# A linear-recurrence attention ahead of two expert layers: a redrawn order of the attention's steps, and inputs laid out time step first

## The chip, the cores and the metric

The kernel runs on one core of a Trainium2 chip. The metric is the device time of one execution in microseconds (us). The engines in the profile are PE (matrix multiplies; PEld its weight loads), DVE (vector), ACT (scalar, activations), POOL (GpSimd) and SP, which here only issues DMA transfers.

## The reference

Three parts run one after the other; the output of each is the next one's input.

```python
def _attn_ref(q, k, v, a_re, a_im):          # each (4, 8, 768, 48): batch, head, time, channel
    mag = np.sqrt(a_re * a_re + a_im * a_im)
    scale = np.minimum(mag, 0.999) / (mag + 1e-06)
    a_re_n, a_im_n = (a_re * scale, a_im * scale)
    for t in range(S):                       # a recurrence over 768 time steps
        new_re = ar * S_re - ai * S_im
        new_im = ar * S_im + ai * S_re
        S_re, S_im = (new_re + k_t v_t^T, new_im)
        y[:, :, t] = q_t S_re
```

Then `x`, the result as 3072 tokens of 384 values, goes through two mixtures of experts: each token takes the one of 8 experts with the highest gate value, `gate * (relu(x @ w1[e]) @ w2[e])`, with `w1` 384 x 1024 and `w2` 1024 x 384. The second layer's gate has a bias that depends on the token's modality.

## The kernel before

**Tiling.** The recurrence is computed in chunks of 128 time steps, as a masked product: within a chunk the decays become cumulative sums of logarithms and angles (matrix multiplies with a triangular matrix, L233), q and k are scaled by the resulting factors, and q k^T under a mask times v gives the chunk's part; a 112-row state `st` carries the rest to the next chunk. Two chunks of one batch element (all 8 heads, 2 x 384 = 768 columns) make a unit; there are 12 units, three for each batch element. Tiles have 128 partitions (time steps) and 384 columns for a chunk or 768 for a unit.

**Steps.** A unit's work is cut into named steps. Those that the text speaks of:
- `ldar`, `ldai`, `ldq`, `ldk`, `ldv` load the inputs by SP's DMA queue (L187); `ck` (L192), `sq1`, `sq3`, `ad` (L202), `su` (L214), `lh`/`ll` (L218 to L221), `th`/`tl` (L228, L230), `tt` (L208) turn the decay into logarithm and angle, 768 columns at a time;
- `pT`, `pL` are the cumulative sums on PE (L233), `fi` and `f` take the angle's fraction (L242, L245), `cf` a few corner rows of it (a cast, L261, and a subtraction, L262);
- `qR` and `kR` scale q and k by the magnitudes (L265, L267), 768 columns;
- `hqc`, `hqs`, `hkc`, `hks` multiply q and k by cosine and sine (L280), 384 columns, with the chunk's number 0 or 1 behind the name. In the trace they are `qhb<-q,fi` (hqc), `qhb<-q,f` (hqs), `khb<-k,fi` (hkc) and `khb<-k,f` (hks);
- `Tq`, `Tk` transpose on PE, `eq`, `ek` copy the results (L168 on ACT, L169 on DVE), `sc` forms the scores, `A` multiplies them by the mask on DVE (L298), `py` and `pu` multiply by v (L304 to L315), `S` and `Sr` keep the state (L322, L347);
- `xe` copies py, `pt` transposes it back, `ye` copies that into `yt`, `st_` stores `yt` into x in DRAM by SP (L1092), `lg` reduces the gate values (L1094).

The router of the first expert layer already works beside the attention: batches of tokens (among others `r1acc`, an addition of 8 columns, L476), and after the last one the finish (`rfnt` to `rfbf`, L498 to L502, and on to the index tile `r1idg`, L521), from which the first gather of tokens `xg` on POOL (L762) follows. `ckon` (L1266) is a memset on DVE for a final check; it waits until all stores into x have landed. Also beside the attention, weights of the experts are loaded (`ws`, L741) and split into two 16-bit parts, and dense work for tokens whose expert was guessed runs on PE with the copies `hh` on ACT (L829) and `hl` on DVE (L830).

**What sets the order.** Nothing is scheduled by the compiler in this part. Each step has a number in the table `AT`, to which the unit's number is added; units 0, 1, 10 and 11 have numbers of their own in `AT_OF`. All steps of all units are sorted by it and issued in that order, so each engine's queue, and SP's, is that order cut down to its own steps. An engine executes its queue in order and waits at an instruction whose input isn't there. Unit 0's wide steps are split into halves, `a` and `b`. The table `ENG` says which engine a step runs on where there is a choice: A is ACT, V is DVE, P is POOL.

```python
todo.append((n+AT_OF.get(n,{}).get(nm,AT[nm]),n,nm,f))
...
todo.sort(key=lambda t:t[:3])
```

Of the kernel before, what the change touches and what calls it, by code (L numbers as in the profile page):

```python
# [18 lines left out]
B, H, S, D = 4, 8, 768, 48  # L19
P = 128  # L20
DM = H * D
# [22 lines left out]
    sub=-59.2026, lhb=-59.0997, zw1=-59.0382, zk0=-53.3853, ldqb=-53.3816, kRa=-53.3802, atb=-50.9528, thb=-50.9075, tlb=-50.8802, llb=-50.8716,
    zw2=-50.8688, aba=-48.2571, zw3=-47.5465, ldkb=-45.6871, csa=-45.6746, sna=-45.6585, qRa=-45.6266, abb=-41.2423, zld=-36.0444, csb=-35.4916,
    zw4=-33.8895, snb=-33.8869, ldva=-32.3857, qRb=-28.9291, zk1=-28.5196, zk3=-22.0775, kRb=-20.8793, zk2=-20.375, zwh7=-20.0527, ldvb=-7.6984,
    zwh5=-7.0878, zwh6=-6.1043, ldar=-4.03, zf=-3.5878, ldai=-3.4105, ck=-3.4097, sq1=-3.0855, sq3=-2.9701, ad=-2.6001, ln1=-2.5145, ln2=-2.5138,
    ex3=-2.5125, ex2=-2.4717, su=-2.4082, tt=-2.3592, lh=-2.0144, at=-1.9704, ll=-1.6353, pL0=-1.6327, th=-1.6191, ldq=-1.6042, tl=-1.5858,
    pT0=-1.5524, R0=-1.547, fi0=-1.5398, Ri0=-1.5358, ldv=-1.5354, f0=-1.5216, pL1=-1.5124, pT1=-1.5111, R1=-1.4687, ldk=-1.4045, Ri1=-1.4044,
    fi1=-1.4016, f1=-1.3988, re=-1.1695, cf=-0.9722, qR=-0.971, ab=-0.9699, sn=-0.6365, kR=-0.6337, hks0=-0.6029, hqs0=-0.585, cs=-0.5549,  # L50
    hkc0=-0.5545, hks1=-0.547, hqs1=-0.5433, Tk0=-0.5359, hqc0=-0.5358, Tq0=-0.535, eq0=-0.5124, hkc1=-0.5034, ek0=-0.4694, Tq1=-0.4692, Tk1=-0.4092,
    sc0=-0.4087, hqc1=-0.4036, eq1=-0.4019, ek1=-0.357, A0=-0.3524, Tq2=-0.105, pu0=-0.0199, sc1=-0.0183, pu1=0.0293, Tk2=0.0293, eq2=0.0298,
    py0=0.03, A1=0.0301, zj=0.1705, ek2=0.3622, Tq3=0.3643, py1=0.3651, S0=0.4002, Tk3=0.4007, xe0=0.4077, sc2=0.4092, eq3=0.4092, pu2=0.4188,
    A2=0.4237, ek3=0.4453, pt0=0.4456, pu3=0.4519, ye0=0.4527, sc3=0.4528, lg0=0.4598, py2=0.4639, A3=0.4672, py3=0.4998, xe1=0.5527, S1=0.6012,
    pt1=0.6448, lg1=1.0276, Sr=1.029, st_0=1.0298, ye1=1.4024, dn0=1.5026, st_1=1.9808, dn1=2.6018, zwl6=2.6952, zwh0=9.4349, zx=18.5444, dn2=19.7371,
# [4 lines left out]
    zl1=146.621, zv3=157.976, zn1=162.009, zn2=187.836, zb1=246.1, zn3=246.175, zy=248.185, zp0=248.274, zp1=248.392, zp2=248.534, zp3=248.627,  # L60
    zp4=248.734,)
# [5 lines left out]
        hqs1=-28.8059, eq0=-20.0658, ek0=-19.7488, hqc1=-13.3169, Tq1=-7.6642, pu0=-7.358, pu1=-7.3535, eq1=-6.3712, Tk1=-3.3378, hks1=-3.3077,
        hkc1=-2.9415, S0=-2.7488, ek1=-1.9123, sc0=-1.5685, A0=-1.5614, Tq2=-1.2232, pu2=-1.2102, Tk2=-1.1192, eq2=-1.1182, pu3=-1.115, py0=-1.1141,
        ek2=-1.1137, sc1=-1.1023, A1=-1.0178, Tk3=-0.9703, Tq3=-0.566, ek3=-0.5563, eq3=-0.5149, sc2=-0.5143, A2=-0.5059, py1=-0.4989, xe0=-0.4897,
        sc3=-0.4333, pt0=-0.2777, A3=-0.1413, ye0=0.057, py2=0.1636, py3=0.198, lg0=0.3641, xe1=0.3867, S1=0.4533, Sr=0.4645, pt1=0.5068, lg1=0.5952,  # L70
# [1 line left out]
    1: dict(
        ldar=-122.2447, ck=-118.7214, ldai=-111.041, sq1=-68.5471, ln2=-60.0846, ex2=-56.9239, sq3=-53.2917, ad=-52.0168, tt=-51.9253, at=-47.9791,
        th=-46.6208, ln1=-42.588, ex3=-37.3201, su=-36.2627, lh=-36.1864, tl=-34.871, ll=-34.321, pT0=-34.3209, fi0=-34.3127, pL0=-29.9243,
        f0=-29.9203, R0=-29.5866, Ri0=-22.4378, pL1=-19.6401, R1=-18.0473, Ri1=-16.2534, pT1=-8.6717, fi1=-8.4218, f1=-8.219, ldk=-7.2703,
        ldq=-4.4455, ab=-2.7035, cf=-2.5673, kR=-2.5652, cs=-2.5614, qR=-2.4893, hkc0=-2.2758, sn=-2.225, re=-2.1309, hqs1=-2.0421, hks0=-1.9986,
        hqs0=-1.9704, Tk0=-1.5026, hkc1=-1.5001, ldv=-1.449, ek0=-1.4431, hqc0=-1.4378, Tq0=-1.4305, Tk1=-1.4192, hqc1=-1.4097, hks1=-1.4083,
        eq0=-1.3907, Tq1=-0.8344, ek1=-0.8342, eq1=-0.8097, Tk2=-0.6367, sc0=-0.5888, Tq2=-0.5863, pu0=-0.5203, A0=-0.5192, py0=-0.4913, eq2=-0.4082,
        ek2=-0.4032, Tq3=0.0297, sc1=0.0338, Tk3=0.0387, A1=0.0388, py1=0.3043, xe0=0.4126, eq3=0.4157, S0=0.4162, sc2=0.4256, pt0=0.4496, A2=0.4516,
        pu2=0.4518, ek3=0.4519, sc3=0.457, py2=0.4689, A3=0.4875, py3=0.5219,),  # L80
    10: dict(
        Ri0=-1.5539, ab=-0.9712, eq0=-0.4979, Tk0=-0.4053, ek0=-0.1036, Tk1=0.0277, sc0=0.7494, Tq1=0.7519, pu0=0.7567, ek1=1.4627, A0=1.6015,
        eq1=1.8231, Tk2=1.8243, sc1=1.8248, Tq2=1.9627, py0=4.4609, A1=6.4672, eq2=6.7564, ek2=6.9082, py1=7.0288, Tq3=8.272, sc2=11.6037,
        pu1=11.7032, xe0=11.7276, Tk3=12.5124, eq3=13.1036, ek3=13.1527, S0=13.3673, A2=13.4097, pt0=15.0475, ye0=15.1973, sc3=15.2236, A3=15.2358,
        py2=17.428, pu2=17.4299, lg0=17.4308, py3=18.0597, pu3=26.4085, xe1=26.4185, S1=26.4723, pt1=26.4802, ye1=26.4873, lg1=26.5282, st_0=30.2202,
        Sr=31.9702, st_1=53.6001,),
    11: dict(
        sq3=-3.3998, fi0=-1.536, Ri0=-1.4981, pT1=-1.4279, fi1=-1.2243, pL1=-1.0127, f1=-0.9962, R1=-0.2456, Ri1=0.4687, ab=0.5224, qR=0.5385,
        kR=0.8233, sn=0.8234, cs=1.9193, hqs0=10.7193, hqc0=12.1152, hkc0=12.3445, Tq0=12.503, hks0=12.504, hkc1=13.7743, eq0=13.9012, Tq1=14.1402,
        hqs1=14.177, Tk0=16.9149, ek0=16.9526, eq1=17.0015, hqc1=17.0187, Tq2=25.408, Tk1=25.4086, eq2=25.4698, Tq3=25.5518, sc0=25.5652, pu0=29.219,  # L90
        ek1=29.2192, hks1=29.2197, A0=29.22, Tk2=29.2205, ek2=30.1283, sc1=30.4591, Tk3=31.0328, A1=31.0793, py0=33.9283, sc2=35.3688, pu1=35.4882,
        A2=36.5036, ek3=36.6086, eq3=37.448, py1=37.6666, sc3=38.0008, S0=39.3703, A3=39.3853, xe0=41.3988, pt0=43.479, py2=48.1531, py3=50.2777,
        xe1=51.5924, ye0=51.792, lg0=52.4969, pt1=52.5183, lg1=55.2838, dn0=62.7472, ye1=68.3041, st_0=72.5776, st_1=72.6059, dn1=72.7172, dn2=78.7804,),
# [1246 lines left out]
```

## Time and profile before

| | |
|---|---|
| three runs | 785.13, 785.62 (the median) and 2927.37 us |
| the profiled execution | 784.11 us, span 782.4 us |
| busy over the span | PE 730.3 us (93%), PEld 584.0, DVE 532.9 (68%), ACT 470.1 (60%), POOL 293.1 (37%) |
| DMA | 159260 packets, 91.40 MB, 131804 of the packets under 512 bytes |
| granted clock of PE, mean | 0.981 |

[...] Idle time stands with what ended it, `<-`. L12 is line 12 of the kernel. [...] The first mask multiply of unit 0 starts at 39.68 us, the last `py` ends about 268.0; these two cut the trace into the three stretches used below.

### The profile page before, as it was taken

To read this page: it belongs to the slowest core of one execution; us is meant where nothing else is said; L and a number is where in the kernel's file an instruction comes from. 1 tells how busy PE (TensorE), PEld (TensorE's weight loads), DVE (VectorE), ACT (ScalarE), POOL (GpSimd) and SP (SyncE) were. 2 spreads that over 40 slices of the span, in tenths; PEclk is the share of its full clock that TensorE was granted. 3 is DMA by queue.
4 is the path that set the end of the run, shared out by engine and by line. 5 is a ranking of instruction groups with operands and counts; after the bars stand their busy time and mean duration, and the time that the engine had idled before them with its cause. 6 is when DMAs were issued, how large, how long until landed. Compare 5 with 4: busy or idle time off the path is not lost. (4 is left out here: it accounts for less than half of the span.)

```text
span 782.4 us, 23426 instructions
## 1 busy us (share of the span) xinstructions
PE 730.3 (93%) x8451; PEld 584.0 (75%) x8451; DVE 532.9 (68%) x1415; ACT 470.1 (60%) x1007; POOL 293.1 (37%) x289
## 2 busy tenths in 40 slices
...
GB/s 220 223 149 220 163 159 165 123 164 96 69 70 62 120 146 94 140 134 114 160 87 175 62 196 78 119 103 204 19 59 188 52 53 44 216 49 43 57 49 30
DMA packets 159260, 91.40 MB, mean 117 GB/s; under 512 B 131804, under 2 KB 149764, under 8 KB 159104
## 3 DMA queue, kind: packets, MB, share of 16 engines
...
HBM read 192.54 MB, written 20.84 MB: 273 GB/s over the span
## 5 line engine op out<-in xcount | busy, mean ns | idle before, releaser
L825 PEld LDWEIGHTS <-wh 128*128 128x128 f16 x1296 | 127.3, 98 | 10.9 <-ACTq L891 3.0
L826 PEld LDWEIGHTS <-wh 128*128 128x128 f16 x1296 | 127.3, 98 | 7.3 <-issue 0.5
L827 PEld LDWEIGHTS <-wl 128*128 128x128 f16 x1296 | 127.3, 98 | 0.0
L846 POOL DMA_INDIRECT x<-yo,r1ids x27 | 28.4, 1052 | 191.7 <-ACT hh L829 81.0
L749 DVE SCALAR_TENSOR_TENSOR wl<-ws,wh 128x768 f16<-128x768 f32 x88 | 83.8, 962 | 14.2 <-ACT wh L748 6.7
L748 ACT ACTIVATE wh<-ws 128x768 f16<-128x768 f32 x88 | 74.4, 851 | 10.0 <-ACTq L861 4.8
L838 PEld LDWEIGHTS <-hl 128*128 128x128 f16 x432 | 42.2, 98 | 44.9 <-DVE hl L830 9.5
L838 PE MATMUL mpy<-wh,hl 128*128 128x384 f16 x216 | 70.6, 327 | 3.5 <-DVE hl L830 1.3
L838 PE MATMUL mpu<-wh,hl 128*128 128x384 f16 x216 | 70.5, 327 | 2.7 <-DVE ev L842 1.1
L836 PE MATMUL mpu<-wh,hh 128*128 128x384 f16 x216 | 70.5, 326 | 0.7 <-ACT hh L829 0.6
L836 PE MATMUL mpy<-wh,hh 128*128 128x384 f16 x216 | 70.5, 326 | 0.0
L837 PE MATMUL mpy<-wl,hh 128*128 128x384 f16 x216 | 70.4, 326 | 0.0
L837 PE MATMUL mpu<-wl,hh 128*128 128x384 f16 x216 | 70.4, 326 | 0.0
L846 POOL DMA_INDIRECT out_dram<-yo,r2ids x21 | 21.0, 1002 | 130.1 <-ACT yo L845 115.9
L825 PE MATMUL msc<-xh,wh 128*128 128x128 f16 x384 | 68.5, 221 | 0.9 <-ACTq L891 0.9
L825 PE MATMUL mpk<-xh,wh 128*128 128x128 f16 x384 | 68.0, 220 | 1.3 <-ACTq L891 1.3
L826 PE MATMUL msc<-xl,wh 128*128 128x128 f16 x384 | 68.4, 220 | 0.0
L827 PE MATMUL msc<-xh,wl 128*128 128x128 f16 x384 | 68.4, 220 | 0.0
L830 DVE SCALAR_TENSOR_TENSOR hl<-mpq,hh 128x256 f16<-128x256 f32 x73 | 30.9, 423 | 54.7 <-ACTq L861 21.8
L827 PE MATMUL mpk<-xh,wl 128*128 128x128 f16 x384 | 68.1, 220 | 0.0
L826 PE MATMUL mpk<-xl,wh 128*128 128x128 f16 x384 | 68.0, 220 | 0.0
L825 PE MATMUL mpq<-xh,wh 128*128 128x128 f16 x384 | 67.6, 219 | 0.0
(512 smaller groups left out, 2259.8 us busy)
## 6 DMA issues: line engine op xcount, KB each, us to landing
...
```

The costliest lines, as they stand in the source:

```text
L748: nc.scalar.activation(H_,S_,AF.Copy,scale=WS,accum_out=s.fl[:,s.n:s.n+1]); s.n+=1
L749: if lo: nc.vector.scalar_tensor_tensor(L_,S_,WS,H_,op0=ALU.mult,op1=ALU.subtract)
L825: nc.tensor.matmul(o,W.h1[:,d,fs],x.h[:,d,:],start=(d==0),stop=False)
L826: nc.tensor.matmul(o,W.h1[:,d,fs],x.l[:,d,:],start=False,stop=False)
L827: nc.tensor.matmul(o,W.l1[:,d,fs],x.h[:,d,:],start=False,stop=(d==ND-1))
L830: def hl(q=q): nc.vector.scalar_tensor_tensor(hs[q][2],hs[q][0][:,:,:P],0.0,hs[q][1],op0=ALU.max,op1=ALU.subtract)
L836: nc.tensor.matmul(o,hh[:,r,:],W.h2[:,f,:],start=(f==0),stop=False)
L837: nc.tensor.matmul(o,hh[:,r,:],W.l2[:,f,:],start=False,stop=False)
L838: nc.tensor.matmul(o,hl[:,r,:],W.h2[:,f,:],start=False,stop=(f==NF-1))
L846: nc.gpsimd.indirect_dma_start(out=s.dst,out_offset=bass.IndirectOffsetOnAxis(ap=R.ids[:,j:j+1] if ids is None else ids(),axis=0),in_=y,in ...
```

## The change

1. The five inputs q, k, v, a_re, a_im are handed over as (batch, time, head, channel) instead of (batch, head, time, channel). A load of 128 time steps thus reads 128 rows of 8 x 48 floats (1536 bytes) instead of 128 x 8 rows of 192 bytes. A step's chunks (two in units 1 to 11, one in unit 0's halves) come in one transfer.
2. All numbers in `AT` and `AT_OF` are new. `RING`, `BATCH`, `WARM` stay.
3. In `ENG`, `hkc1`, `hks1`, `hqc1`, `kR` and, in unit 0, `kRb` and `ttb` go from POOL to DVE; `ek1` goes from DVE to ACT and `xe0` from ACT to DVE; `ye0` goes from DVE to ACT and `ye1` from ACT to DVE.
4. A second form of the attention behind a branch (`gen_attention`), which is not taken here, reads the new layout too.

```diff
@@ -37,60 +37,60 @@
 AT=dict(
-    zq3=-275.454, ldarb=-264.9366, zq2=-255.701, ckb=-255.2219, ldara=-254.8635, sq1b=-254.7775, cka=-246.2329, ln2b=-245.3372, sq1a=-186.1661,
...
+    zq3=-158.0658, ldarb=-158.0658, ldara=-158.0657, ldaia=-158.0657, zq2=-156.761, ckb=-156.2861, sq1b=-154.5986, ln2b=-154.0208, zq4=-153.7814,
...
@@ -99,9 +99,9 @@
 ENG=dict(
-    ek2="A", ek3="A", eq0="A", eq1="A", eq2="A", eq3="A", lh="A", sq1="A", sq1a="A", sq3="A", xe0="A", xe1="A", ye1="A", Sr="P", hkc0="P", hkc1="P",
-    hks0="P", hks1="P", hqc1="P", hqs0="P", hqs1="P", kR="P", kRa="P", kRb="P", qR="P", tt="P", ttb="P", ek0="V", ek1="V", hqc0="V", lha="V", lhb="V",
-    qRa="V", qRb="V", sq1b="V", sq3a="V", sq3b="V", th="V", tha="V", thb="V", tta="V", ye0="V",)
+    ek1="A", ek2="A", ek3="A", eq0="A", eq1="A", eq2="A", eq3="A", lh="A", sq1="A", sq1a="A", sq3="A", xe1="A", ye0="A", Sr="P", hkc0="P", hks0="P",
+    hqs0="P", hqs1="P", kRa="P", qR="P", tt="P", ek0="V", hkc1="V", hks1="V", hqc0="V", hqc1="V", kR="V", kRb="V", lha="V", lhb="V", qRa="V", qRb="V",
+    sq1b="V", sq3a="V", sq3b="V", th="V", tha="V", thb="V", tta="V", ttb="V", xe0="V", ye1="V",)
@@ -183,8 +183,8 @@
         def load(nm, src, bufs):
             def ld(_,s,sl):
                 if not hasattr(u,nm): setattr(u,nm,inp.tile([P,HC,H,D],F32,name=nm,tag=nm,bufs=bufs))
-                for c in range(sl.start//DM,sl.stop//DM):
-                    nc.sync.dma_start(out=getattr(u,nm)[:,c],in_=src[b,:,(c0+c)*P:(c0+c+1)*P,:].rearrange("h p d -> p h d"))
+                i,e=sl.start//DM,sl.stop//DM
+                nc.sync.dma_start(out=getattr(u,nm)[:,i:e],in_=src[b,(c0+i)*P:(c0+e)*P].rearrange("(c p) h d -> p c h d",p=P))
@@ -1325,6 +1325,9 @@
     for name in _INS:
...
+        if name in _INS[:5]:
+
+            a = _np.ascontiguousarray(a.transpose(0, 2, 1, 3))
```

How the order moves is seen best where an engine's instructions stand. POOL first, in the middle of the attention: two stretches of one unit each, before

```order
L208 TENSOR_TENSOR x_996<-ai,x_996 128x768
L265 TENSOR_TENSOR q<-q,Rb_154 128x768
L267 TENSOR_TENSOR k<-k,Ri 128x768
L280 TENSOR_TENSOR khb_153<-k,f 128x8x48
L280 TENSOR_TENSOR qhb_150<-q,f 128x8x48
L280 TENSOR_TENSOR khb_153<-k,fi 128x8x48
L280 TENSOR_TENSOR khb_151<-k,f 128x8x48
L280 TENSOR_TENSOR qhb_148<-q,f 128x8x48
L280 TENSOR_TENSOR khb_151<-k,fi 128x8x48
L280 TENSOR_TENSOR qhb_148<-q,fi 128x8x48
```

and with the change:

```order
L208 TENSOR_TENSOR x_1386<-ai,x_1386 128x768
L347 TENSOR_TENSOR st_1368<-st_1368,re 112x384
L265 TENSOR_TENSOR q<-q,Rb_154 128x768
L280 TENSOR_TENSOR khb_151<-k,f 128x8x48
L280 TENSOR_TENSOR khb_151<-k,fi 128x8x48
L280 TENSOR_TENSOR qhb_148<-q,f 128x8x48
L280 TENSOR_TENSOR qhb_149<-q,f 128x8x48
```

The wide multiply k (L267) and three of the seven multiplies of L280 are gone from POOL's unit; the number behind a name tells the tiles of a name apart. They stand on DVE now. A piece of DVE's unit before

```order
L242 TENSOR_SCALAR fi<-pT 128x384
L280 TENSOR_TENSOR qhb_148<-q,fi 128x8x48
L298 TENSOR_TENSOR A<-psc,mask 128x512
L245 TENSOR_TENSOR f<-pT,fi 128x384
L169 COPY kT<-pk 112x512
```

and with the change:

```order
L242 TENSOR_SCALAR fi<-pT 128x384
L245 TENSOR_TENSOR f<-pT,fi 128x384
L280 TENSOR_TENSOR khb_152<-k,fi 128x8x48
L280 TENSOR_TENSOR khb_152<-k,f 128x8x48
L280 TENSOR_TENSOR qhb_149<-q,fi 128x8x48
L214 SCALAR_TENSOR_TENSOR x_1782<-x_1782,x_1772 128x768
L242 TENSOR_SCALAR fi<-pT 128x384
L298 TENSOR_TENSOR A<-psc,mask 128x512
```

Three multiplies in a row stand where one stood, ahead of the mask multiply. The third place is the end of the attention, on SP. Before:

```order
L1092 DMA x<-yt 128x384 x2
L741 DMA ws_90<-in_moe_w_dram 128x3x1024
L1092 DMA x<-yt 128x384 x2
L741 DMA ws_91<-in_moe_w_dram 128x8x384
```

With the change:

```order
L1092 DMA x<-yt 128x384 x2
L741 DMA ws_90<-in_moe_w_dram 128x3x1024
L741 DMA ws_91<-in_moe_w_dram 128x8x384
L1092 DMA x<-yt 128x384
```

The last store of the attention has moved behind both weight loads. The copy that feeds it was on ACT (`ye1`) and is now on DVE, with the change:

```order
L830 SCALAR_TENSOR_TENSOR hl<-mpq,hh 128x256
L169 COPY yt<-pt 128x384
L498 TENSOR_SCALAR rfnt<-mpT 128x8
```

It stands behind the last `hl` and ahead of the router's finish, in which `ckon` has moved from ahead of `rfnt` (L498) to behind `rfbf` (L502).

## Rows read from the trace of the kernel before

**Rows 1.** The same execution in stretches: length, busy time and instructions by engine, PEclk, DMA share, GB/s.

```profile
0.00:39.68 39.68, 27.43 (x175) 14.21 (x176) 35.15 (x73) 32.18 (x50) 22.79 (x48) 0.91 1.10 219
39.68:268.00 228.32, 211.05 (x2450) 177.22 (x2448) 197.06 (x366) 190.65 (x296) 153.33 (x117) 0.96 0.61 126
268.00:782.40 514.40, 491.78 (x5833) 392.61 (x5829) 300.68 (x977) 247.31 (x662) 116.96 (x124) 0.99 0.32 105
```

**Rows 2.** Largest wait of PE, 40 to 260 us: total us, times, longest.

```profile
PE pr L339 <- DVE rtrk L478: 5.9, 2, 2.9
```

**Rows 3.** Stretches again, of two units (from a unit's first mask multiply to the next's).

```profile
97.40:118.23 20.83, 19.61 (x241) 16.09 (x240) 20.20 (x35) 18.58 (x29) 15.50 (x12) 1.00 0.74 159
158.16:179.22 21.06, 19.78 (x242) 16.15 (x240) 20.01 (x34) 19.21 (x29) 13.79 (x12) 1.00 0.92 174
```

**Rows 4.** The tile q: durations in ns, min/median/max.

```profile
L280 DVE TENSOR_TENSOR qhb<-q,fi x12: 543/674/1346, 25.7 to 245.0; 128x384 f32<-128x384 f32 x12
```

**Rows 5.** Timeline of DVE around 85 us: start, us, instruction.

```profile
84.69 0.95 DVE L221 SCALAR_TENSOR_TENSOR ll<-x,lh 128x768 f16<-128x768 f32 x1
85.56 0.55 DVE L228 TENSOR_SCALAR th<-x 128x768 f16<-128x768 f32 x1
```

**Rows 6.** Groups of POOL's instructions, 39.68 to 268 us: busy us, mean ns | idle before.

```profile
L280 POOL TENSOR_TENSOR khb<-k,f 128x384 f32<-128x384 f32 x22 | 24.9, 1130 | 29.9 <-ACT f L157 20.0 <-issue 10.0
L280 POOL TENSOR_TENSOR khb<-k,fi 128x384 f32<-128x384 f32 x22 | 24.2, 1100 | 9.4 <-ACT fi L157 7.3 <-PE pu L315 2.1
L267 POOL TENSOR_TENSOR k<-k,Ri 128x768 f32<-128x768 f32 x10 | 19.6, 1959 | 0.0
L280 POOL TENSOR_TENSOR qhb<-q,fi 128x384 f32<-128x384 f32 x11 | 11.8, 1072 | 0.0
```

**Rows 7.** Timelines of POOL and DVE at 82 us, of DVE at 141.

```profile
81.42 1.82 POOL L267 TENSOR_TENSOR k<-k,Ri 128x768 f32<-128x768 f32 x1
81.95 1.52 DVE L261 CAST cfb<-f 32x384 f16<-32x384 f32 x1
...
140.87 0.36 DVE L261 CAST cfb<-f 32x384 f16<-32x384 f32 x1
```

**Rows 8.** Timelines of POOL and DVE at 135 us, of DVE at 273.

```profile
137.04 1.79 POOL L267 TENSOR_TENSOR k<-k,Ri 128x768 f32<-128x768 f32 x1
135.25 3.62 DVE L476 TENSOR_TENSOR r1acc<-r1acc,rtsu 128x8 bf16<-128x8 bf16 x1 [0.87 <-PE pr L473]
...
272.99 0.17 DVE L476 TENSOR_TENSOR r1acc<-r1acc,rtsu 128x8 bf16<-128x8 bf16 x1
```

**Rows 9.** Groups of DVE's instructions, 39.68 to 268 us.

```profile
L202 DVE CUSTOM_DVE_ANT_0 x<-x,x 128x768 f32<-128x768 f32 x10 | 11.8, 1179 | 1.2 <-ACT x L195 1.2
L228 DVE TENSOR_SCALAR th<-x 128x768 f16<-128x768 f32 x10 | 7.0, 702 | 2.0 <-ACT x L157 2.0
L280 DVE TENSOR_TENSOR qhb<-q,fi 128x384 f32<-128x384 f32 x11 | 8.5, 773 | 0.0
L261 DVE CAST cfb<-f 32x384 f16<-32x384 f32 x6 | 6.6, 1095 | 0.1
L476 DVE TENSOR_TENSOR r1acc<-r1acc,rtsu 128x8 bf16<-128x8 bf16 x4 | 8.9, 2226 | 1.9 <-PE pr L473 1.7
```

**Rows 10.** Timeline of DVE at the start.

```profile
3.91 0.55 DVE L192 TENSOR_SCALAR_CACHE_REDUCE x<-ar 128x384 f32<-128x384 f32 x1 [1.33 <-DMA ar<-in_a_re_dram]
```

**Rows 11.** The page's line on the DMA packets.

```profile
DMA packets 159260, 91.40 MB, mean 117 GB/s; under 512 B 131804, under 2 KB 149764, under 8 KB 159104
```

**Rows 12.** Timelines of DVE and ACT at the end of the attention.

```profile
270.56 0.48 ACT L168 COPY yt<-pt 128x384 f32<-128x384 f32 x1 [0.83 <-DVE r1lg L1094]
...
275.53 0.41 DVE L830 SCALAR_TENSOR_TENSOR hl<-mpq,hh 128x256 f16<-128x256 f32 x1
276.74 0.17 DVE L1266 MEMSET ckon<- 128x128 f32 x1 [0.79 <-DMA x<-yt]
...
278.39 0.23 DVE L502 TENSOR_TENSOR rfbf<-rfky 128x64 f32<-128x64 f32 x1
```

More of the change, by code (lines that the diff above doesn't have):

```diff
@@ L44 @@
[L44 to L55, printed above, removed]
@@ new lines @@
+    Tk0=-0.0497, ek0=-0.0261, Tq0=-0.0258, hkc1=-0.0255, Tk1=-0.0255, hks1=-0.0254, hqs1=-0.004, hqc1=0.0343, eq0=0.0517, ek1=0.0708, Tq1=0.0808,
+    sc0=0.0821, Tk2=0.1266, pu0=0.1269, A0=0.1278, pu1=0.1364, zj=0.1705, eq1=0.1928, Tq2=0.1966, sc1=0.197, eq2=0.3421, A1=0.3421, py0=0.3468,
+    Tq3=0.3677, ek2=0.3682, Tk3=0.3684, sc2=0.3786, eq3=0.4183, ek3=0.4228, py1=0.423, A2=0.4233, S0=0.4317, xe0=0.432, sc3=0.9495, py2=0.9506,
+    pu2=0.9519, A3=0.9742, py3=0.9746, pu3=0.994, S1=1.0438, xe1=1.1608, Sr=1.3421, pt0=1.3436, ye0=1.3814, lg0=1.4206, pt1=1.4321, lg1=1.9742,
@@ new lines @@
+    dn0=1.9744, ye1=2.1574, st_0=2.2234, st_1=2.4162, zwl6=2.6952, dn1=3.2036, zwh0=9.4349, zx=18.5444, dn2=19.4475, zwh2=22.9948, zwh4=25.1415,
+    zec0=27.4267, zwh1=27.8833, zec1=31.1581, zec2=32.499, zes0=36.406, zes1=39.3171, zb0=40.2, zes2=40.4556, zwl0=40.4969, zg0=43.5134, zwl2=44.0341,
+    zwl5=46.1229, zg1=46.5527, zwh3=47.1601, zs0=48.8419, zwl7=49.0052, zt0=50.3089, zwl4=50.9329, ze=51.2097, zT0=56.3585, zc0=56.6477, zs1=61.8791,
+    zl0=62.3709, zm0=63.218, zt1=63.7944, zwl1=65.9349, zh0=67.4886, zv0=71.8316, zm1=78.3957, zm2=80.9205, zh1=81.4287, zwl3=83.2655, zm3=86.1353,
@@ L67 @@
[L67 to L70, printed above, removed]
@@ L71 @@
-        ye1=1.3291, st_0=1.3673,),
-    1: dict(
[L73 to L80, printed above, removed]
@@ L81 @@
-    10: dict(
[L82 to L86, printed above, removed]
@@ L87 @@
-    11: dict(
[L88 to L93, printed above, removed]
+        pT0=-72.852, pL0=-72.6845, fi0=-72.1216, R0=-71.0185, f0=-70.9475, Ri0=-65.7237, pT1=-64.1229, fi1=-41.8572, pL1=-41.4051, hks0=-41.2023,
@@ new lines @@
+        hkc0=-41.1897, hqs0=-40.898, f1=-40.7965, hqc0=-31.3145, R1=-30.8257, Tk0=-30.429, Tq0=-25.9357, ek0=-25.9255, re=-25.9188, cf=-25.9185,
+        Ri1=-25.8479, Tk1=-25.8336, eq0=-25.791, Tq1=-22.5209, eq1=-22.4828, sc0=-22.4603, ek1=-1.8049, pu0=-1.8043, A0=-1.8042, hkc1=-1.804,
+        hks1=-1.7925, pu1=-1.6285, sc1=-1.3069, py0=-1.295, hqc1=-1.2677, Tk2=-1.2554, hqs1=-1.0097, ek2=-0.8774, A1=-0.8774, Tq2=-0.8773,
+        py1=-0.8753, Tk3=-0.8735, S0=-0.8661, eq2=-0.866, Tq3=-0.8656, xe0=-0.807, sc2=-0.8067, A2=-0.8063, pu2=-0.4297, eq3=-0.3875, ek3=-0.022,
@@ new lines @@
+        pt0=-0.0111, sc3=-0.0044, py2=0.1206, pu3=0.1281, A3=0.134, py3=0.17, ye0=0.3554, lg0=0.3843, S1=0.4233, Sr=0.4299, xe1=1.0305, pt1=1.0846,
+        lg1=1.189, st_0=1.9586, ye1=1.9618,),
+    1: dict(
+        ldai=-73.9897, sq3=-73.4205, ldar=-65.1343, ck=-63.8118, sq1=-63.7846, ad=-42.8849, ln2=-42.8721, ln1=-42.0859, ex2=-41.8585, tt=-32.7779,
+        ex3=-26.9178, su=-26.8832, at=-26.7937, th=-26.7856, lh=-23.6643, tl=-23.4919, ll=-23.4607, pT0=-23.4602, pL0=-23.4601, fi0=-23.46,
+        f0=-3.1597, pT1=-3.13, Ri0=-2.8047, R0=-2.8042, fi1=-2.8041, f1=-2.7963, cf=-2.7868, pL1=-2.786, Ri1=-2.5858, ab=-2.5134, sn=-2.385,
+        ldk=-2.2651, cs=-1.8682, kR=-1.8672, ldq=-1.866, hks0=-1.8482, hkc0=-1.8062, R1=-1.8029, qR=-1.4694, re=-1.0678, hqc0=-1.0354, hqs0=-0.9967,
+        Tk0=-0.9585, Tq0=-0.9117, ek0=-0.8831, hqs1=-0.8751, hqc1=-0.8628, hkc1=-0.8308, eq0=-0.7547, Tk1=-0.658, ldv=-0.5997, Tq1=-0.5766,
+        hks1=-0.5765, sc0=-0.5765, A0=0.0304, pu0=0.0304, ek1=0.0489, eq1=0.0489, Tk2=0.049, py0=0.049, sc1=0.1324, Tq2=0.1898, A1=0.194, ek2=0.2093,
+        Tk3=0.3421, eq2=0.3423, py1=0.3667, ek3=0.3709, Tq3=0.3983, eq3=0.4263, sc2=0.4271, S0=0.6193, xe0=0.6316, pu2=0.6418, A2=0.6752, py2=0.6883,
+        sc3=0.9558, A3=0.9742, py3=1.0304, pt0=1.1897,),
```

43 lines of the change are left out of this document (29 added, 14 removed).

## The prediction

> **What bounds the kernel now.** I read the stretches first [rows 1]. The program falls into a start without any mask multiply (0 to 39.68 us), the attention proper (39.68 to 268.0) and the two expert layers (268.0 to 782.4). The reader should see that only the middle one is contested: PE is busy 211.05 of 228.32 us (92%), DVE 197.06 (86%), ACT 190.65 (84%), POOL 153.33 (67%). The last stretch holds the same instructions before and after, with PE busy 491.78 of 514.40 us, so what the attention gains or loses moves the end one to one, unless the join between the two costs something (below).
>
> Next, what PE waits for in the attention [rows 2]: of its 228.32 - 211.05 = 17.3 us of idle time the largest part, 5.9 us in two waits, is for a result of DVE (rtrk, the router's), and six of the next seven groups of waits, each 0.7 to 2.1 us, name DVE too. Then the attention unit by unit [rows 3]. In the densest stretches PE is idle 1.2 to 1.3 us and DVE only 0.6 to 1.1 us (20.20 of 20.83 and 20.01 of 21.06: idle 3.0% and 5.0%). So PE and DVE both sit at the limit, and **DVE's load decides the period of a unit**.
>
> **What DVE is given.** The change moves four steps a unit from POOL to DVE: three multiplies of 128x384 (hkc1, hks1, hqc1) and one of 128x768 (kR). The swaps ek1/xe0 and ye0/ye1 exchange copies of equal shape between DVE and ACT and cancel. Units 1 to 11 have 33 such multiplies and, in this stretch, 10 wide ones. An undisturbed 128x384 multiply on DVE took 543 ns at least [rows 4], so 0.55; an undisturbed wide instruction 0.95 [rows 5], and the next one starts 0.08 us before its predecessor's record ends (84.69 + 0.95 against 85.56). That is 33 x 0.55 + 10 x 0.95 - 43 x 0.08 = 24.3 us. Unit 0's halves add 5 x (0.55 - 0.08) = 2.4. DVE's busy time up to 268 goes from 35.15 + 197.06 = 232.2 to **258.9 us**. POOL loses a third of the qhb multiplies' 11.8, half of khb's 24.9 and 24.2, and the wide k multiply's 19.6 [rows 6]: about 56 of 153 us; what stays is 0.63 of it.
>
> **What DVE wins back.** Much of DVE's busy time is waiting that its records hide. The wide multiply k on POOL ran from 81.42 to 83.24, the cast on DVE from 81.95 to 83.47; an undisturbed cast took 0.36 [rows 7]. Of the six casts four stood so. The addition r1acc started at 135.25 and ended at 138.87, just when two wide POOL instructions in a row were done (138.83); alone it takes 0.17 [rows 8]. Each group's excess over its undisturbed time, times its count [rows 9]: five groups of ten wide steps, of which ad (0.23 each) is the first and th (0.15) the last, 9.0 together; qhb 11 x 0.22 = 2.5, casts 6 x 0.735 = 4.4, r1acc 4 x 2.06 = 8.2. Together **24.1 us**.
>
> After the change this lies between two ends. Lower end: none, if the new order keeps such steps away from POOL's. Upper end: all of it stays, and the 43 new multiplies, which read two tiles as qhb does, wait as qhb and ad do now: 33 x 0.22 + 10 x 0.23 = 9.6, so 34. I take a value in between, by kind. All four slow casts and three of the r1acc stood against the wide k multiply, which leaves POOL: casts 0, r1acc 8.2 less two times 1.8 = 4.6. The other 11.5 and the new 9.6 shrink with POOL's work: 21.1 x 0.63 = 13.3. Sum 17.9. DVE then has 258.9 - 24.1 + 17.9 = 252.7 us. With the idle share of its densest unit, 3.0%, and 3.9 us before its first input is there [rows 10], attention ends at 252.7 / 0.97 + 3.9 = 264.4, against 268.0: **-3.6**. At 5% idle it would be 269.9, +1.9.
>
> [...]
>
> **The loads.** 120 transfers of 1024 pieces of 192 bytes become 65 (unit 0's two chunks stay apart) with 128 rows of 1536 bytes a chunk: of 159,260 packets 120 x 1024 = 122,880 go and 15,360 come, leaving about 51,740 [rows 11]. But hardly anybody waits for them: the one wait that counts is DVE's 1.33 us at the very start [rows 10]. The cover is that a unit's tiles are loaded a unit ahead. The price lies between 0 and -1.3 us; I take half, **-0.7**. Were the cover gone, the wait would be for the landing of one load, and that has an eighth of today's pieces for the same bytes. The start itself is otherwise work moved from one side of 39.68 to the other: 0.
>
> **The join.** The last yt copy now ends on ACT at 271.04, its store is issued then, and the wait of ckon on DVE for the last store ends at 276.74 [rows 12]. In the new order the copy stands on DVE behind the hl that ends at 275.94, so it is ready near 276.4, and its store stands on SP behind both weight loads. With the same 5 to 6 us from store to landing it lands near 282. DVE meets ckon at 278.6, after rfbf; queued behind it are rfnb and the rest of the router's finish, on which r1idg and the first gather wait. Lost are about 282 - 278.6 = 3.4 us, less what that chain has to spare. PE has dense work of its own until about 288, so 0 to +5; I take **+3**.
>
> Sum: -3.6 - 0.7 + 3.0 = -1.3. The profiled execution took 784.11 us (span 782.4 and 1.7 around it); it goes to 782.8. The runs' median, 785.62, lies 1.5 higher, so **784 us**: no change. Faster or slower by 2% means 15.7 us, under 769.9 or over 801.3, about what a measurement of this kernel can tell from no change.
>
> **Rivals.**
> 1. *DVE's waits vanish and PE's clock rises.* Then DVE needs (258.9 - 24.1) / 0.97 + 3.9 = 246.0 and PE becomes the bound: 39.68 + 211.05 = 250.7, or 241.6 at the full clock throughout (0.96 was granted). Attention ends near 250, -18, the join costs 0 to 3: **768 us** (764 to 771). For it: more than half of the hidden waits (12.6 of 24.1) are casts and r1acc, and most of those stood against the one wide step that leaves POOL. Against: DVE would have to be idle 3% while loaded 12% more. Chance 0.24.
> 2. *DVE becomes the bound (slower).* The multiplies meet POOL's and wait, or POOL's remaining four a unit come late and hold DVE. With the waits unshrunk (24) at 4% idle attention ends at 258.9 / 0.96 + 3.9 = 273.6, +5.6; at 34 and 5% idle at (258.9 + 9.6) / 0.95 + 3.9 = 286.5, +18.5; with +3 and the median that is 794 and 807, priced at **800 us**. It decides from where DVE's hidden waits exceed 19.1 us: (234.8 + 19.1) / 0.97 + 3.9 = 265.7, which with the other two terms is today's time. For it: DVE is already 95 and 97% busy in the dense units. Against: POOL's share falls to 97 of 228 us, 0.42. Chance 0.21. [...]
> 3. *Nothing moves, because PE stays the bound and all of this is hidden* (PE loses no instruction and the order only shifts its gaps): **786 us**. Chance 0.13. That the change doesn't do what it says can only concern the loads (packets stay near 159,000); as nobody waits for them, it gives the same time and is counted here.
>
> The forecast has 0.42. Of rival 1 some 0.20 lies under 769.9, of the forecast's spread 0.03; of rival 2 0.11 lies over 801.3, of the forecast's 0.02. **Faster 0.23, same 0.64, slower 0.13.** The range 766 to 800 leaves out about the lower third of rival 1 and the upper half of rival 2, some 0.2.
>
> **What would show it.** Right: packets near 51,700; POOL near 97 us in the attention; DVE near 252 up to the last attention step and 95% or more busy in every unit; casts of f near 0.36 and r1acc below 2 us; the last store landing near 282 with a wait of ckon of 3 us. Rival 1: DVE's groups at their undisturbed means, PE without waits for DVE. Rival 2: the new multiplies at 0.8 us or more, units over 21 us, PE waiting for khb, qhb or the mask multiply. I am wrong if the weight loads, given free DMA time, move something in the last stretch, or if PE's clock falls further as its gaps close: 2% less clock over 211 us is 4 us.

## The result and the profile after

The changed kernel took **773.04 us** (median of 4 runs, 772.39 to 773.94), the kernel before 785.38 beside it; the ratio is **0.9862** with the interval 0.9819 to 0.9906. The ratio leaves out the one run of 2927.37 us of the kernel before, so it is not the quotient of the two medians. The time lies in the range, 11 us below the forecast's 784 and 5 above rival 1's 768. The gain is less than 2%, but its interval excludes "no change". The profiled execution took 772.39 us, span 770.7.

The same three stretches of the trace after, cut at the first mask multiply (32.5) and the last py (248.5); columns as in [rows 1]:

```profile
0.00:32.50 32.50, 23.34 (x124) 11.47 (x125) 26.09 (x70) 26.15 (x39) 14.68 (x41) 1.00 0.78 267
32.50:248.50 216.00, 205.05 (x2498) 176.27 (x2497) 198.47 (x424) 194.74 (x307) 104.81 (x75) 0.98 0.42 135
248.50:770.70 522.20, 493.01 (x5833) 395.13 (x5829) 300.37 (x973) 247.28 (x661) 115.81 (x124) 0.99 0.31 102
```

The attention ends at 248.5, 19.5 us earlier; the rest, with the same 5833 PE instructions, takes 522.2 us where it took 514.4. So 19.5 us were won and 7.8 given back. PE is now busy 95% of the middle stretch, DVE still 92%.

Where PE stood still before is best seen in stretches of 6 us. The kernel before at its two stops, columns as in [rows 1]:

```profile
132.00:138.00 6.00, 4.18 (x48) 3.76 (x47) 5.13 (x6) 5.36 (x9) 5.75 (x4) 1.00 0.96 228
138.00:144.00 6.00, 4.87 (x39) 4.40 (x40) 4.08 (x11) 2.31 (x4) 0.84 (x1) 0.52 0.97 130
192.00:198.00 6.00, 5.18 (x54) 4.22 (x52) 5.14 (x9) 5.37 (x10) 5.15 (x4) 1.00 0.70 134
198.00:204.00 6.00, 3.88 (x35) 3.41 (x36) 4.70 (x10) 3.29 (x4) 1.83 (x2) 0.64 0.20 30
```

The changed kernel in two of the same stretches:

```profile
132.00:138.00 6.00, 6.00 (x94) 5.59 (x89) 5.72 (x17) 5.97 (x10) 0.96 (x1) 1.00 0.68 198
138.00:144.00 6.00, 6.00 (x66) 5.08 (x65) 6.00 (x12) 5.97 (x10) 4.83 (x5) 1.00 0.80 296
```

Before, PE stops for rtrk [rows 2], from 136.2 to 139.1 and from 197.2 to 200.1 us, and the granted clock (PEclk, 1.00 being full speed), 1.00 in the stretch in which a stop begins, is 0.52 and 0.64 in the one in which it ends. After, PE is busy 11.87 us or more in every 12 from 72 to 228. Its largest waits between 32 and 249 us come before 60 us, in the first units, and none is for rtrk:

```profile
PE pL L233 <- ACT Rb L157: 2.9, 1, 2.9
PE pL L233 <- ACT Ri L157: 1.7, 1, 1.7
PE psc L295 <- ACT kT L168: 1.6, 1, 1.6
```

DVE's groups after, 32.5 to 248.5 us, answer to [rows 9] (the wide k and the khb multiplies are the ones that came from POOL):

```profile
L280 DVE TENSOR_TENSOR qhb<-q,fi 128x384 f32<-128x384 f32 x23 | 12.8, 558 | 0.9 <-POOL q L265 0.9
L202 DVE CUSTOM_DVE_ANT_0 x<-x,x 128x768 f32<-128x768 f32 x10 | 11.2, 1117 | 0.0
L267 DVE TENSOR_TENSOR k<-k,Ri 128x768 f32<-128x768 f32 x11 | 10.5, 955 | 0.7 <-ACT Ri L157 0.5
L280 DVE TENSOR_TENSOR khb<-k,fi 128x384 f32<-128x384 f32 x12 | 8.5, 705 | 0.0
L280 DVE TENSOR_TENSOR khb<-k,f 128x384 f32<-128x384 f32 x12 | 6.6, 548 | 0.0
L228 DVE TENSOR_SCALAR th<-x 128x768 f16<-128x768 f32 x10 | 5.6, 556 | 0.7 <-ACT x L157 0.5
L261 DVE CAST cfb<-f 32x384 f16<-32x384 f32 x7 | 2.5, 356 | 0.2
L476 DVE TENSOR_TENSOR r1acc<-r1acc,rtsu 128x8 bf16<-128x8 bf16 x4 | 0.7, 170 | 0.4
```

On the mean casts, r1acc, th, the wide k and two of the three moved groups run at their undisturbed durations (0.36, 0.17, 0.55, 0.95 and 0.55 us [rows 4, 5, 7, 8]); some of ad and khb<-k,fi still take longer (up to 1775 ns where the shortest took 948, and up to 952 against 548). POOL's groups, against [rows 6]:

```profile
L280 POOL TENSOR_TENSOR khb<-k,f 128x384 f32<-128x384 f32 x11 | 15.6, 1417 | 58.0 <-DVE k L267 29.7 <-ACT f L157 20.6 <-PE psc L295 7.7
L280 POOL TENSOR_TENSOR khb<-k,fi 128x384 f32<-128x384 f32 x11 | 11.0, 997 | 0.0
```

POOL now waits for DVE's wide k 29.7 us in all and takes 1417 ns for khb<-k,f where it took 1130. It has the time: it is busy 104.81 of 216.00 us.

The packets came as forecast, and DVE's waits for its first input did not go (1.33 us before [rows 10], 0.68 + 0.83 after, the second in a half that was not late before):

```profile
DMA packets 50861, 91.39 MB, mean 119 GB/s; under 512 B 8045, under 2 KB 41365, under 8 KB 50705
```

```profile
3.25 0.55 DVE L192 TENSOR_SCALAR_CACHE_REDUCE x<-ar 128x384 f32<-128x384 f32 x1 [0.68 <-DMA ar<-in_a_re_dram]
5.24 0.55 DVE L192 TENSOR_SCALAR_CACHE_REDUCE x<-ar 128x384 f32<-128x384 f32 x1 [0.83 <-DMA ar<-in_a_re_dram]
```

The join, against [rows 12]: the last copy, the wait for its store, and the index tile that the first gather needs. (Two names that follow are new: `eyo` and `yo` are the tiles with the expert layers' results, `eyo` of the guessed tokens and `yo` of the others; POOL stores them, and the time of such a store is its start.)

```profile
256.14 0.55 DVE L169 COPY yt<-pt 128x384 f32<-128x384 f32 x1
...
260.66 0.17 DVE L1266 MEMSET ckon<- 128x128 f32 x1 [1.61 <-DMA x<-yt]
...
265.15 0.19 DVE L521 TENSOR_SCALAR r1idg<-mpt 128x31 int32<-128x31 f32 x1 [0.76 <-PE mpt L518]
```

r1idg comes 17.9 us earlier (283.08 before). Of the 7.8 us given back, 1.6 are thus lost ahead of r1idg, where ckon now waits 1.61 us (0.79 before). Another 4.1 go between the second store of eyo and the first of yo (15.2 us before, 19.3 after; "the segment" below), at the branch behind r1idg (L891). ACT's sequencer there, the kernel before and then the changed one:

```profile
L891 ACTq EVENT_SEMAPHORE  x2: 17/17/17, 291.3 to 291.4; - x2
L891 ACTq COMPARE_BRANCH  x1: 74/74/74, 290.8 to 290.8; - x1
```

```profile
L891 ACTq EVENT_SEMAPHORE  x2: 17/17/17, 276.1 to 276.2; - x2
L891 ACTq COMPARE_BRANCH  x1: 74/74/74, 273.0 to 273.0; - x1
  PE mpk L825: 4.0, 1
```

From the branch to the next event ACT takes 0.5 us before and 3.1 after, and PE waits 4.0 for it (1.3 before). The last 2.1 us are lost at the program's final branch, where DVE waits 3.77 us instead of 1.57. From the last store to the end the changed kernel takes 8.1 us (again in e7), the kernel before 6.0; e2, with the new order and engines, takes 6.4 and e4, in the old order, 8.4. So it goes neither with the order nor with the engines; its cause stays open.

### The profile page after: what moved, and what is told of

It reads as the page before. It is cut to its first block, busy times and chain, and to the rows that moved or that the text cites. A ratio compares the mean times of both kernels' runs of the same rounds, so it can differ in the third digit from the quotient of the medians.

```text
span 770.7 us, 23364 instructions
## 1 busy us (share of the span) xinstructions
PE 721.4 (94%) x8451; PEld 582.9 (76%) x8451; DVE 524.9 (68%) x1464; ACT 468.2 (61%) x1007; POOL 235.3 (31%) x240
## 2 busy tenths in 40 slices
DMA packets 50861, 91.39 MB, mean 119 GB/s; under 512 B 8045, under 2 KB 41365, under 8 KB 50705
## 5 line engine op out<-in xcount | busy, mean ns | idle before, releaser
L825 PEld LDWEIGHTS <-wh 128*128 128x128 f16 x1296 | 127.7, 99 | 13.6 <-ACTq L891 5.7
L827 PE MATMUL mpq<-xh,wl 128*128 128x128 f16 x384 | 67.6, 219 | 0.0
L826 PE MATMUL mpq<-xl,wh 128*128 128x128 f16 x384 | 67.6, 219 | 0.0
```

Source lines behind the costliest of these rows:

```text
L825: nc.tensor.matmul(o,W.h1[:,d,fs],x.h[:,d,:],start=(d==0),stop=False)
L826: nc.tensor.matmul(o,W.h1[:,d,fs],x.l[:,d,:],start=False,stop=False)
L827: nc.tensor.matmul(o,W.l1[:,d,fs],x.h[:,d,:],start=False,stop=(d==ND-1))
```

## The experiments

Theory A says that the new order took away waits that DVE's records hid. Counted up to r1idg on DVE, each instruction against the shortest with the same operation, tiles and shape in all fourteen traces, the hidden waits were 44.8 us before and 11.8 after (the 13.6 in the expectation of e3 is a first count, from the first trace of the changed kernel). Theory F came after the first four runs: what counts is whether PE stops. "PE idle" is r1idg's time less PE's busy time. The last three columns come from one profiled execution of each kernel; the two of the changed kernel (after and e7) differ by 1.4 us in r1idg.

| kernel | median us | before, same chip | ratio, interval | r1idg us | PE busy / idle | DVE hidden |
|---|---|---|---|---|---|---|
| before | 785.38 | | | 283.1 | 252.9 / 30.2 | 44.8 |
| after | 773.04 | 785.38 | 0.9862, 0.9819 to 0.9906 | 265.2 | 242.8 / 22.4 | 11.8 |
| e1 new loads alone | 795.20 | 785.35 | 1.0121, 1.0062 to 1.0179 | 285.8 | 253.7 / 32.1 | 44.9 |
| e2 old loads | 770.54 | 785.35 | 0.9822, 0.9774 to 0.9870 | 265.7 | 242.9 / 22.8 | 11.4 |
| e3 old engines | 794.78 | 785.35 | 1.0111, 1.0064 to 1.0157 | 293.4 | 254.7 / 38.7 | 45.6 |
| e4 old order | 798.84 | 785.35 | 1.0163, 1.0097 to 1.0230 | 294.2 | 257.2 / 37.0 | 28.8 |
| e8 before, rank first | 781.09 | 785.67 | 0.9954, 0.9916 to 0.9991 | 280.8 | 252.7 / 28.1 | 43.9 |
| e9 after, stalls | 775.49 | 785.67 | 0.9860, 0.9827 to 0.9894 | 272.1 | 248.8 / 23.3 | 12.0 |
| e5 after, early store | 771.18 | 785.67 | 0.9805, 0.9769 to 0.9841 | 263.8 | 245.2 / 18.6 | 11.8 |
| e7 after again | 774.62 | 785.67 | 0.9853, 0.9823 to 0.9884 | 266.6 | 245.7 / 20.9 | 12.7 |
| e12 before, r1acc on POOL | 767.26 | 776.66 | 0.9863, 0.9820 to 0.9906 | 270.4 | 249.3 / 21.1 | 38.8 |
| e6 new loads, sgn later | 782.96 | 776.66 | 1.0079, 1.0051 to 1.0106 | 284.3 | 254.5 / 29.8 | 45.1 |
| e10 after, late hint | 762.85 | 776.66 | 0.9819, 0.9777 to 0.9861 | 263.6 | 242.9 / 20.7 | 11.7 |
| e11 e10 with old loads | 762.34 | 776.66 | 0.9806, 0.9765 to 0.9846 | 266.0 | 246.3 / 19.8 | 11.7 |

The last four ran on a chip on which the expert layers are some 6 us shorter (first to last store of the first layer 244 us against 249) and the attention is not (e10 and e5 have r1idg at 263.6 and 263.8); their ratios are to the kernel before on that chip, and the times named in their expectations are meant for the others.

**e1, new loads alone.** The changed kernel with the old tables:

```diff
-AT=dict(zq3=-158.0658, ...   ENG=dict(ek1="A", ...
+AT=dict(zq3=-275.454, ...    ENG=dict(ek2="A", ...
```

> The kernel before with the new layout and one transfer a unit alone; order and engines are the old ones. [...] Rival B (the start became shorter, 39.68 to 32.5 us, because the loads stopped filling the DMA engines): the first mask multiply comes near 33 us and the time falls by some 7 us, to 778.

Theory A, in which the loads are hidden, has no change here, 785 us within 2; rival B has 778. Neither came: it is 1.2% slower. The first mask multiply stays at 39.6 us, so the loads did not make the start. sgn, an instruction outside of the written order, had been put 12 rows earlier on DVE:

```profile
46.45 0.18 DVE L1140 TENSOR_SCALAR sgn<-mi 128x24 f32<-128x24 int32 x1 [3.63 <-DMA mi<-in_moe_modality_id_dram]
```

**e2, old loads.** The kernel before with the two new tables.

```diff
-AT=dict(zq3=-275.454, ...    ENG=dict(ek2="A", ...
+AT=dict(zq3=-158.0658, ...   ENG=dict(ek1="A", ...
```

> The changed kernel with the old layout and two transfers a unit; the new order and engines stay. Theory A: 773 us within 2, first mask multiply near 32.5. Rival B: the start's 7 us come back, 780 us. A third case, that the new order issues loads so late that it needs them cheap: DVE, ACT or POOL wait for DMA in the attention by more than 5 us, and the time is over 780.

The whole gain is there without the loads (first mask multiply at 32.6), so rival B falls; theory A's 773 within 2 is missed by 0.5 us on the fast side. e2's gain is no smaller than the change's.

**e3, old engines** and **e4, old order**: the changed kernel with one of its two tables set back.

```diff
-ENG=dict(ek1="A", ...   hkc1="V", hks1="V", hqc0="V", hqc1="V", kR="V", ...
+ENG=dict(ek2="A", ...   hkc1="P", hks1="P", hqc1="P", kR="P", ...
```

> The changed kernel (new order, new loads) with the old table of engines: kR, hkc1, hks1 and hqc1 on POOL again. Theory A: POOL's busy time in the attention returns from 105 to some 150 us, DVE loses 27 us of work and gets hidden waits back, some 30 us in place of 13.6, and the units stretch where POOL's steps come late: 780 to 800 us. Rival C (the order alone made the gain, the engines don't matter): 773 us within 3.

```diff
-AT=dict(zq3=-158.0658, ...
+AT=dict(zq3=-275.454, ...
```

> The old order with the new engines and the new loads. Theory A (the moves pay only in an order that keeps DVE's two-input steps clear of POOL's): DVE carries 27 us more, the casts and r1acc lose some 12 us of waits, other waits stay: 785 to 800 us, hidden waits of DVE over 20 us. Rival D (the moves themselves take the waits away, whatever the order): 776 us or less, hidden waits under 15.

In both runs theory A's range of times holds, and rivals C and D fall. Against e1, which shares their loads, the order alone gives nothing (794.8 against 795.2), the engines alone nothing (798.8), and together 22 us (773.0). At r1idg each alone is some 8 us later than e1. Theory A's other number for e3 is missed: hidden waits of 45.6 us, not some 30. In e4 the moves did take 16 us of hidden waits away, yet r1idg is 11 us later than before, and r1acc still waits at two places (2.44 us each). So the sum of DVE's waits does not tell the time. Nor does DVE's load alone: its durations up to r1idg sum to 268.8 us before, 283.7 in e4, where the load may well be the reason, but 269.6 in e3, which is as late.

**e8, rank first.** In the router's batch of the kernel before:

```diff
-        su=T([P,E],"su"); nc.vector.tensor_reduce(out=su, ...
-        nc.vector.tensor_add(s.acc,s.acc,su)
         rk=T([P,n,E],"rk"); nc.vector.scalar_tensor_tensor(rk,pr ...
         r=T([P,n],"r",bufs=5); nc.vector.tensor_reduce(out=r,in_=rk, ...
+        su=T([P,E],"su"); nc.vector.tensor_reduce(out=su, ...
+        nc.vector.tensor_add(s.acc,s.acc,su)
```

> The kernel before, with one change in the router's batch: rtrk and rtr, for which PE waits, stand ahead of rtsu and r1acc on DVE instead of behind them. DVE does the same work, and r1acc still waits some 3.4 us for POOL at the same two places. Theory F (what counts is whether PE stops: two stops of 2.9 us for rtrk, each followed by a stretch at a lower clock, 0.52 of full speed from 138 to 144 us and 0.64 from 198 to 204): the stops and the dips after them go, PE's busy time up to r1idg falls by 4 to 6 us, and the time falls by 6 to 11 us, to 775 to 780. Theory G (DVE's load decides the units' period, as predicted): no change, 785 within 2.

A small gain (0.5%; 4.6 us at the median), below F's 6 us and more than G's nothing; three of its five runs took 781 us and two 786, and the trace is of one of the latter. The wait for rtrk went and another came up in its place, PE's largest in 40 to 260 us now:

```profile
PE psc L295 <- DVE A L298: 7.1, 5, 2.5
```

The mask multiply stands behind the blocked r1acc too (3.0 us long here, twice). The stop moved to the next instruction in DVE's queue, and the clock still fell (0.72 from 138 to 144 us, 0.55 from 198 to 204).

**e12, r1acc on POOL.** The kernel before, with a step dn3 that adds on POOL, behind the wide k (the second layer's router still adds on DVE, by a line left out here):

```diff
-        nc.vector.tensor_add(s.acc,s.acc,su)
+        s.pend=lambda: nc.gpsimd.tensor_add(s.acc,s.acc,su)
...
+            st["dn3"]=lambda: flags.pend()
```

> The kernel before with the router's addition r1acc taken from DVE to POOL, behind the wide multiply k that it had to wait for; order and engines of all else stay. Theory F: DVE no longer stands still for 3.4 us at 135 and 196 us, so PE's two stops go, whichever instruction stood behind r1acc, with the clock's dips after them: r1idg 6 to 11 us earlier (272 to 277 us), the time 774 to 780. If the stops only find another cause, as with rtrk placed first (r1idg 2.3 us earlier), not more than that: 781 to 785.

This speaks for F. r1idg comes at 270.4, 12.7 us earlier, more than F's 6 to 11, and the ratio, 0.9863, is that of the whole change. In the stretches of the stops:

```profile
132.00:138.00 6.00, 6.00 (x66) 4.94 (x65) 5.10 (x12) 5.25 (x9) 5.29 (x4) 1.00 0.90 224
138.00:144.00 6.00, 6.00 (x90) 4.96 (x88) 5.89 (x10) 5.60 (x10) 3.57 (x5) 1.00 1.20 173
192.00:198.00 6.00, 6.00 (x94) 5.01 (x94) 5.89 (x11) 5.58 (x8) 3.28 (x4) 1.00 0.39 61
198.00:204.00 6.00, 6.00 (x58) 5.37 (x57) 5.78 (x12) 5.97 (x10) 6.00 (x5) 1.00 0.40 105
```

PE never stops there, and the clock stays at 1.00, while five casts of 1.2 to 1.7 us and most other hidden waits are still there (38.8 of 44.8 us): r1acc's 8.2 went and 2.2 came elsewhere. DVE's durations up to r1idg sum to 262.0 us, 6.8 less than before. So by DVE's load, or by the length of its waits, 6 to 7 us were to be won, and 12.7 came: 9.1 of PE's idle time and 3.6 of its busy time. What cost was 3.4 us in one piece, twice.

**e9, stalls put into the changed kernel.**

```diff
+        if imv is None and i0 in (0,6):
+            for _ in range(4): nc.vector.tensor_tensor(out=s.boh[:,sl,:], ... ,op=ALU.is_equal)
         rk=T([P,n,E],"rk"); nc.vector.scalar_tensor_tensor(rk,pr ...
```

> The changed kernel with four needless 128x768 comparisons (0.96 us each undisturbed, 3.8 together) on DVE ahead of rtrk in two of the router's batches, near 135 and 187 us, where PE is never idle now. Theory F: PE stops at both places or soon after, the granted clock falls below 0.9 for some 6 us behind each stop, and the time rises by more than the 7.6 us that DVE got, to 781 to 787. If PE's stops cost only themselves: at most 7.6 us, 773 to 781, and the clock stays at 1.00.

Mixed. The stalls were shorter than planned: four comparisons took 2.33 us together at each of the two places, so DVE got 4.7 us and not 7.6.

```profile
136.96 2.33 DVE L479 TENSOR_TENSOR r1boh<-io 128x768 f16<-128x768 f16 x4
```

r1idg comes 5.5 us later than in e7. The total is 775.49 against e7's 774.62, which is no clear difference; it lies below theory F's range and in that of stops that cost only themselves. PE stops for 1.6 us at both places; the clock falls behind one of them only:

```profile
138.00:144.00 6.00, 4.25 (x45) 3.49 (x46) 5.85 (x14) 5.76 (x9) 0.96 (x1) 1.00 0.97 346
192.00:198.00 6.00, 4.73 (x40) 4.45 (x40) 5.89 (x13) 4.55 (x7) 1.24 (x1) 0.72 0.31 110
```

Had the stops cost only themselves, r1idg would have come 3.3 us later, the sum of PE's waits for rtrk. The 5.5 are more than that, but two traces of one kernel differ by 1.4. What decides whether a stop brings a dip isn't settled. Nor does a run show that the changed kernel's own gain comes from r1acc alone: e12 shows what the block cost in the kernel before, and putting stalls back was not clear in the time.

**e5, early store**, and **e7**, the changed kernel once more.

```diff
-        ... dn2=79.8585, ye1=236.022, st_0=237.649,
-        st_1=237.6867,),
+        ... dn2=79.8585, ye1=61.2, st_0=61.25,
+        st_1=61.3,),
```

> The changed kernel with the last yt copy and its store at their old places in the order: the copy right behind the last gate reduction on DVE, the store ahead of the second weight load on SP. The wait of ckon (1.6 us) goes, r1idg comes 1.6 us earlier, near 263.5 us. If the join passes it on, the time falls by 1.6 us; if the 4 us that ACT and PE lose at the branch behind r1idg are a matter of when it comes, anything from -4 to +2.

> The changed kernel once more, for comparison on the same chip: 773 us within 2. If the 4 us behind r1idg (19.3 us between the second eyo scatter and the first yo scatter instead of 15.2) and the 2.1 us at the very end come again, they belong to the order; if not, they are the spread between executions.

ckon no longer waits (it stands at 255.93 with no idle time before it), r1idg is 2.7 us earlier than in e7 (1.3 than in the first trace of the changed kernel), and the ratio is 0.9805 against 0.9853: the intervals overlap, the median is 3.4 us lower. In e7 the segment took 20.2 us, in e5 19.2, in e2 and e9 19.1, and 15.2 to 15.3 in before, e1, e3, e4, e6 and e8: the 4 us belong to the new order with the new engines. The 2.1 us at the very end came again in e7 too, but not in e2 or e5 (6.4 and 6.8 us from the last store to the end), which share its order and engines but for one copy and its store in e5.

**e10 and e11, a later hint**: e5 with the branch's hint moved (the step zb0, which tells the engines of the branch ahead of it), then the same with the old loads.

```diff
-    zb0=40.2,
+    zb0=126.0,
```

> The changed kernel with the early store, and with the hint of the branch behind r1idg (on ACT, SP, DVE and POOL) later: on ACT ahead of the first eyo instead of 16 instructions earlier. If the 3 us that ACT takes from its branch to its next event (0.5 in the kernel before) come from the early hint: 0.5 again, 15.2 us between the second eyo scatter and the first yo scatter in place of 19 to 20, time 767. If not: 771 as with the early store alone.

> As the last one, with the old layout and two transfers a unit. If the new loads bring nothing: within 2 us of the last one. If they cost 2 to 3 us, as the changed kernel with the old loads seemed to show (770.5 against 773.0): 764 to 769.

The hint is not it: ACT still takes 3.2 us behind its branch, the segment 19.1 and 19.3 us. Its cause stays open (in e12, in the old order, the segment took 16.9, with 0.5 us behind ACT's branch). e11 and e10 agree within 0.5 us, so in the new order the loads bring nothing and cost nothing that shows. Against the kernel before, e5, e10 and e11 are the fastest of all (0.9805 to 0.9819), though not clear of the changed kernel's interval.

**e6, sgn later.** e1 with sgn computed in the step ze, at the end of the attention.

```diff
-            nc.vector.tensor_scalar(out=sg,in0=mi[:,:,0],scalar1=-2.0, ...
+                r.update(ze=lambda: (nc.vector.tensor_scalar(out=sg,in0=mi[:,:,0], ...
```

> The new layout and loads alone in the old order, with sgn, which the scheduler had put 12 rows earlier on DVE there and which then waited 3.6 us for its input, late in the attention instead. If that wait was what the layout cost in the attention: attention and r1idg as in the kernel before (268.0 and 283.1 us) and the time back to 785 within 3. If the layout itself slows the expert layers: again 790 or more, with the same r1idg.

The second case: still 0.8% slower than the kernel before, which takes 776.66 on this chip, with r1idg only 1.2 us later. The loss sits at the second layer's branch: 18.6 us between the last eyo store and the first yo store (18.7 in e1, 13.2 before). ACT's sequencer in e6:

```profile
L891 ACTq EVENT_SEMAPHORE  x2: 17/17/17, 591.9 to 592.0; - x2
L891 ACTq COMPARE_BRANCH  x1: 60/60/60, 589.0 to 589.0; - x1
```

2.9 us from branch to event, 0.5 in the kernel before. The last of the changed loads is issued at 219 us, so they are not under way here; again it is the stretch behind a branch, and why it is slow in some kernels and not in others no run here shows.

## Why the prediction was right, and where not

The time came inside the range, but the mechanism was that of rival 1, not the forecast's. The range reached down to 766 and so took in rival 1's 768; that the sum for "no change" stands within it is luck.

- **"DVE's load decides the period of a unit": wrong.** The term was that DVE would be busy 252.7 us up to the end of the attention and set it at 264.4. DVE was busy 26.09 + 198.47 = 224.6 us and the attention ended at 248.5, in rival 1's place (250), with PE as the bound, as rival 1 said. Up to r1idg, PE's busy time fell by 10.1 us (7.2 in e7) at a granted clock that rose from 0.91 to 1.00 in the start and from 0.96 to 0.98 in the attention, and its idle time by 7.8.
- **The hidden waits were mis-sized.** 24.1 us were taken from eight groups; against the shortest of each form there were 36.0 in that stretch and 8.4 ahead of it. The value for after, 17.9, was too high: 11.8 up to r1idg. The work moved was well sized: DVE's undisturbed work up to r1idg went from 224.0 to 255.0, 31.0 us; the forecast's 26.7 is 30.5 when the 0.08 us are added by which each of the 48 overlaps its neighbour. The two cancel: DVE's durations sum to 268.8 before and 266.7 after.
- **That a hidden wait costs its length, wherever it stands: wrong.** This is the step that failed. r1acc's 8.2 us stood in the rows [rows 8, 9], and PE's 5.9 us for rtrk in [rows 2]; what wasn't seen is that these are one chain (POOL's two wide steps, r1acc, rtrk or the mask multiply, PE, then the clock). e12 shows its price in the kernel before: 6.0 us less of hidden waits gave 12.7 us at r1idg, where the forecast gave the whole change 3.6 in the attention. e8 shows that it does not help to put another instruction behind the block.
- **The start, costed at 0:** the first mask multiply came 7.2 us earlier, in e2 as well, so by the order and not by the loads; e12 does not have this (39.6). Work moved across it is a small part on DVE: 73 instructions ahead of it became 70, and undisturbed work 30.0 us became 28.6. The hidden waits there fell from 8.4 us to 1.7; that they held up the mask multiply is likely but no run shows it. The 58 instructions more in the middle stretch (424 for 366) are mostly the 43 multiplies from POOL.
- **The loads, -0.7:** packets as forecast (50,861), nothing gained; alone in the old order the kernel was 0.8 to 1.2% slower (e6, e1), which no term had.
- **The join, +3:** ckon's wait was forecast near 3 us and came as 1.6; r1idg gained 17.9 of 19.5. The branch behind it, 4.1 us, was in no term, nor were the 2.1 us at the end. These losses are why it is 773 and not rival 1's 768.
- **Rival 2** fell for the change: no unit is stretched by DVE. Its slower time is what either table alone gives (795 and 799); in e4 DVE has 14.9 us more of durations, as it said, in e3 not.

The upper end of DVE's waits took the 43 moved multiplies to last as much longer as qhb and ad did before. On the mean the wide k took 955 ns, qhb<-q,fi 558 and khb<-k,f 548, and khb<-k,fi alone, at 705, was longer than undisturbed. The mask multiply took 673 to 693 ns in all 48 instances after, 32 of them beside a POOL step. Before, each of r1acc's three long records (3.62, 3.62 and 1.50 us) ended within 0.04 us of a wide step's end on POOL, and four casts beside one took 1.41 to 1.52 us in place of 0.36 [rows 7]; what holds them up no run shows. What such waits do to the time depends on the order: all eleven wide k multiplies on DVE (945 to 960 ns) stand clear of POOL, and POOL is made to wait instead, the 29.7 us above.
